# A four-layer S5/H3 stack on one core: pairwise scan, convolution first, layers chunk by chunk

## The chip, the cores and the metric

The kernel runs as one launch on one core of a Trainium2 chip. The metric is the device time of the launch in microseconds; several launches are timed and the median is given. TensorE (PE) multiplies matrices into PSUM, VectorE (DVE) and ScalarE (ACT) work on SBUF and PSUM, GpSimd (POOL) makes a few index tables, and SyncE (SP) issues every DMA, in order.

## The reference

Four layers act on x, 2048 tokens of 640 channels in bf16, with a residual each: A, B, A, B. Both A layers share their weights, and so do both B layers.

```python
def _A_ref(x, ...):                       # x is layer-normed: u
    Lam_bar = exp(dt * Lam);  B_bar = ((Lam_bar - 1) / Lam)[:, None] * Bmat
    Bu = einsum("bld,pd->blp", x, B_bar)  # complex, 640 states
    for t in range(L): h = Lam_bar * h + Bu[:, t]
    y = 2 * einsum("blp,dp->bld", hseq, Cmat).real + x * Dskip

def _B_ref(q, k, v, ...):                 # q is layer-normed x
    kv = (4-tap causal filter of k by shift_k) * v
    y = causal convolution of kv with ssm_k along 2048 tokens (by FFT of 4096)
    return q * (y + kv * ssm_D)

x = x + A(layernorm(x)); x = x + B(layernorm(x)); x = x + A(layernorm(x)); x = x + B(layernorm(x))
```

The convolution Y = y + kv * ssm_D does not depend on x: it is computed once and used by both B layers.

## The kernel before

A list scheduler (class `Sched`) is given tasks with engines, estimated durations, dependencies and a priority; it plays them through and emits their instructions in the order of their planned starts. So the order on each engine is fixed in the program and comes from the planner's numbers. Buffers come from `Ring`s whose slots are assigned in the order in which tasks are written down.

The program has two parts, each with its own schedule.

*Part 1* holds the setup of A's weights (`a_setup_tasks`), the DFT tables (`y_table_tasks`), the preparation of kv and of the filter (`kv_tasks`), the convolution, and layer A1, planned together. `kv_tasks` treats 128 channels at a time. k is transposed in by DMA, filtered by four diagonal matmuls (L884), multiplied by v on DVE (L893), and stored to `kvs`. The filter `ssm_k` is transposed in by DMA (L837), rearranged by ACT (L845) and stored to `ksx`. `y_pass_builders` then runs five passes of 128 channels: load K and V by DMA transpose (L993, L1008), stage A (L936), stage B (L964 to L971), the spectral product on DVE (L1030 to L1035), the inverse (L1062 to L1066), a DMA transpose of `q` (L1084), the last inverse step (L1101), and a store to `ysc` (L1116). Evictions go to ACT (L249) or DVE (L251). All passes wait for a task `gate`:

```python
gate = S.add("gate", "pool", 0.0, [AT["bt"], AT["tab"], AT["w"], TK["inv"], TK["fa"]]
             + x_ready + kv_stores + kk_stores, e_gate)
```

*Part 2* loads the whole of Y (L1315) and runs B1, A2 and B2 over x, which stays in SBUF in f32.

Layer A (`a_layer_tasks`) works in chunks, of 256 tokens in A1 and of 512 in A2. LayerNorm: squares on ACT (L489), root (L495 to L500), application on ACT (L509) into `u`. A DMA transpose makes `uT` (L542). PE forms Bu (L557), ACT evicts it to `ab` (L563). The complex recurrence is run as two real scans: Bu is rotated by the angle of Lam_bar (DVE, L579 to L584), scanned, and rotated back into `h` (L625 to L630), with a carry between chunks. The scans are one per 128 states and per real or imaginary part:

```python
for c2 in range(2):
    for j in range(NJ):                                   # NJ = 5
        nc.vector.tensor_tensor_scan(g[:, c2, j, :], r[:, j:j + 1].to_broadcast([P, CH]),
                                     g[:, c2, j, :], init, ALU.mult, ALU.add)   # L594
```

PE multiplies `h` by C (L648), adds the skip by a diagonal matmul (L654) and the residual x by an f32 identity matmul (L657); ACT evicts the sum into x with its row sums (L665). Layer B (`b_apply_tasks`) multiplies the normed x by Y on DVE (L1145) and adds the residual (L1147, or L1150 into the output).

Of the kernel before, what the change touches and what calls it, by code (L numbers as in the profile page):

```python
# [17 lines left out]
P = 128  # L18
# [5 lines left out]
CHMAX = 512  # L24
# [5 lines left out]
HALF_PI = 0.5 * math.pi  # L30

# [10 lines left out]
class Task:  # L42
    __slots__ = ("name", "eng", "engs", "ests", "est", "deps", "emit", "idx", "start", "finish", "rank", "succ", "bias", "lat")

    def __init__(self, name, eng, est, deps, emit, idx, bias, lat):
        if isinstance(eng, (tuple, list)):
            self.engs = tuple(eng)
            self.ests = tuple(float(e) for e in est)
        else:
            self.engs = (eng,)  # L50
            self.ests = (float(est),)
# [6 lines left out]
        self.bias = bias  # L58
        self.lat = lat


class Sched:
    LAT = {"pe": 0.15, "act": 0.25, "dve": 0.2, "pool": 0.3, "sp": 2.0, "sp": 2.0}
# [6 lines left out]
    def add(self, name, eng, est, deps, emit, bias=0.0, lat=None):  # L70
        t = Task(name, eng, est, deps, emit, len(self.tasks), bias, lat)
        self.tasks.append(t)
        return t

    def vis(self, d):
        return d.finish + (d.lat if d.lat is not None else self.LAT.get(d.eng, 0.2))

    def run(self):
        tasks = self.tasks
        for t in tasks:  # L80
            for d in t.deps:
                d.succ.append(t)
        for t in reversed(tasks):
            t.rank = t.est + max((s.rank for s in t.succ), default=0.0) + t.bias
        eng_free = {}
        ndep = {t.idx: len(t.deps) for t in tasks}
# [8 lines left out]
        remaining = len(tasks)  # L95
        all_engs = sorted({e for t in tasks for e in t.engs})
        DMAQ = ()
        while remaining:
            progressed = False
            for eng in all_engs:  # L100
                if eng_free.get(eng, 0.0) > now + 1e-9:
                    continue
                if eng in DMAQ and eng_free.get("bus", 0.0) > now + 1e-9:
                    continue
                cands = [t for t in ready if eng in t.engs and rtime[t.idx] <= now + 1e-9]
                if not cands:
                    continue
                def okay(t):
                    return t.engs[0] == eng or eng_free.get(t.engs[0], 0.0) > now + 0.3
                cands = [t for t in cands if okay(t)]  # L110
# [8 lines left out]
                if eng in DMAQ:  # L119
                    eng_free["bus"] = t.finish  # L120
                order.append(t)
                remaining -= 1
# [8 lines left out]
            nxt = []  # L131
            for t in ready:
                for eng in t.engs:
                    f = eng_free.get(eng, 0.0)
                    if eng in DMAQ:
                        f = max(f, eng_free.get("bus", 0.0))
                    nxt.append(max(f, rtime[t.idx]))
            nxt = [x for x in nxt if x > now + 1e-9]
# [3 lines left out]
        assert len(order) == len(tasks), "dependency cycle"  # L142
        order.sort(key=lambda t: (t.start, t.idx))
        for t in order:
            t.emit()
        self.makespan = max(t.finish for t in tasks) if tasks else 0.0
        if self.debug and tasks:
            busy = {}
            for t in tasks:
                busy[t.eng] = busy.get(t.eng, 0.0) + t.est  # L150
            print("[sched] makespan %.1f  busy: %s" % (self.makespan, {k: round(v, 1) for k, v in busy.items()}))
            byeng = {}
            for t in order:
                byeng.setdefault(t.eng, []).append(t)
            pos = {t.idx: i for e in byeng.values() for i, t in enumerate(e)}
            t = max(tasks, key=lambda t: t.finish)
            chain = []
            while t is not None and len(chain) < 400:
                chain.append(t)
                cands = [(self.vis(d), d) for d in t.deps]  # L160
                i = pos[t.idx]
                if i > 0:
                    pv = byeng[t.eng][i - 1]
                    cands.append((pv.finish, pv))
                cands = [c for c in cands if abs(c[0] - t.start) < 1e-6]
                t = cands[0][1] if cands else None
            chain.reverse()
            last = None
            out = []
            for t in chain:  # L170
                out.append("%s@%.1f" % (t.name, t.start))
            print("[sched] critical chain (%d): %s" % (len(chain), " > ".join(out[:: max(1, len(out) // 60)])))
            bk = 20.0
            nb = int(self.makespan / bk) + 1
            engs = ["pe", "act", "dve", "pool", "sp", "sp"]
            occ = {e: [0.0] * nb for e in engs}
            for t in tasks:
                s0, e0 = t.start, t.finish
                b0 = int(s0 // bk)
                while s0 < e0 - 1e-9:  # L180
                    be = (b0 + 1) * bk
                    seg = min(e0, be) - s0
                    occ[t.eng][b0] += seg
                    s0 += seg
                    b0 += 1
            print("[sched] occupancy per %.0fus (pe act dve pool sp sq):" % bk)
            for b_ in range(nb):
                print("   %5.0f  " % (b_ * bk) + " ".join("%3.0f" % (100 * occ[e][b_] / bk) for e in engs))
        self.tasks = []
        return self.makespan  # L190


class Slot:
    __slots__ = ("tile", "users", "alloc")

    def __init__(self, alloc):
        self.tile = None
        self.users = []
        self.alloc = alloc

    def get(self):
        if self.tile is None:
            self.tile = self.alloc()
        return self.tile


class Ring:

    def __init__(self, bufs, alloc):
        self.bufs, self.alloc, self.slots = bufs, alloc, []  # L210

    def new(self):
        war = list(self.slots[-self.bufs].users) if len(self.slots) >= self.bufs else []
        s = Slot(self.alloc)
        self.slots.append(s)
        return s, war


def t_mm(n, f32=False):
    return (0.45 if f32 else 0.216) * n / 512.0 + 0.012  # L220


def t_act(n, sb=False):
    return 0.30 + (0.00083 if sb else 0.00076) * n


def t_tt(n, slow=False):
    return 0.06 + (0.00108 if slow else 0.00055) * n
# [1168 lines left out]
```

## Time and profile before

| | |
|---|---|
| timed runs | 586.04 us median of 3 (585.99 to 587.17) |
| profiled execution | span 583.7 us; its own time is not listed, so the 2.3 us around the span are taken from the median |
| PE busy | 370.4 us (63%), weight loads beside it 256.7 |
| DVE busy | 394.4 us (68%) |
| ACT busy | 339.1 us (58%) |
| POOL busy | 13.7 us (2%) |
| DMA | 44.81 MB, mean 77 GB/s |
| chain that ended last | DVE 43%, PE 25%, ACT 21%, DMA 6% |
| granted TensorE clock, mean | 0.860 |

In a row of groups stand the source line, engine, operation, written and read tiles, form and count; then busy us and mean ns of one; then the idle time of the engine just before them and what ended it. A slice row has 40 digits, each the busy tenths of a fortieth of the span.

### The profile page before, as it was taken

How to read it: one execution, taken by the hardware profiler on the slowest of the kernel's cores; microseconds unless marked ns; L12 is line 12 of the kernel's file. 1: busy time of each engine (PE TensorE's matmuls, PEld its weight loads, DVE VectorE, ACT ScalarE, POOL GpSimd, SP SyncE). 2: the span in 40 equal slices, each digit the busy share in tenths (PEclk: the TensorE clock that was granted, in tenths of full speed). 3: DMA queues.
4: the chain of work that ended last, by engine and by line, in shares of the span. 5: the costliest groups of instructions: out<-in, count | busy, mean ns of one | idle time of the engine just before them, and what ended most of it. 6: DMA issues, size and time to landing. Idle time of an engine off the chain costs nothing.

```text
span 583.7 us, 8215 instructions
## 1 busy us (share of the span) xinstructions
PE 370.4 (63%) x3233; PEld 256.7 (44%) x3233; DVE 394.4 (68%) x799; ACT 339.1 (58%) x584; POOL 13.7 (2%) x38
## 2 busy tenths in 40 slices
PE   0326557659989898898979510075496793970291
PEld 0225547437767776686766410032153251530050
DVE  5974445992956977868961513559999299729903
ACT  8979964237778755674645419995241621960033
POOL 4211000000000000000000000000000000000000
PEclk9999869889999998998989755577887797995596
DMA  8931898681335451423103154040002002110101
GB/s 256 173 77 47 190 244 201 180 199 37 73 60 108 60 111 24 95 55 79 37 1 73 37 107 182 4 86 2 0 0 46 0 2 45 46 45 0 45 1 45
DMA packets 124370, 44.81 MB, mean 77 GB/s; under 512 B 117543, under 2 KB 122924, under 8 KB 124204
## 3 DMA queue, kind: packets, MB, share of 16 engines
q1 hardware_dynamic: 124332, 44.29, 33.4%
q8 instruction: 25, 0.41, 0.3%
q14 instruction: 13, 0.11, 0.1%
HBM read 9.51 MB, written 10.49 MB: 34 GB/s over the span
## 4 chain that ended last, share of the span: by engine, by line
DVE 43%; PE 25%; ACT 21%; DMA 6%; issue 2%; SPq 2%; POOL 0%; DVEq 0%; ACTq 0%; POOLq 0%
DVE g L594 13%; PE pb L557 7%; PE pc L648 6%; ACT junk L489 6%; ACT q L249 4%; ACT bu L509 3%; PE pc L657 3%; DMA uT<-u 2%; ACT ab L563 2%; DVE bo L1150 2%; DVE g L581 2%; DVE t L579 2%; DVE t L582 2%; DVE t L580 2%; DVE t L626 2%
## 5 line engine op out<-in xcount | busy, mean ns | idle before, releaser
L648 PE MATMUL pc<-W,h 128*128 128x128 bf16 (+1 forms) x640 | 110.2, 316 | 61.5 <-DVE h L627 53.5
L557 PE MATMUL pb<-uT,BT 128*128 128x256 bf16 (+1 forms) x600 | 105.3, 328 | 63.5 <-ACT std L496 37.0
L249 ACT ACTIVATE q<-yps 128x1024 bf16<-128x1024 f32 (+2 forms) x104 | 95.9, 964 | 32.7 <-PE yps L971 16.9
L648 PEld LDWEIGHTS <-h 128*128 128x128 bf16 x640 | 52.9, 101 | 122.8 <-DVE h L627 66.3
L557 PEld LDWEIGHTS <-BT 128*128 128x128 bf16 x600 | 60.2, 103 | 88.3 <-DVE std L495 37.1
L594 DVE TENSOR_TENSOR_SCAN g<-r,ncarry,g 128x256 bf16<-128x256 f32 (+1 forms) x100 | 82.3, 890 | 0.0
L665 ACT ACTIVATE x<-pc 128x640 f32<-128x640 f32 x32 | 22.4, 701 | 97.9 <-PE pc L657 97.8
L489 ACT ACTIVATE junk<-x,nmean 128x640 bf16<-128x640 f32 x64 | 52.2, 816 | 22.3 <-DVE nmean L483 22.3
L563 ACT ACTIVATE ab<-pb 128x512 bf16<-128x512 f32 (+1 forms) x60 | 43.7, 737 | 34.9 <-PE pb L557 15.4
L657 PE MATMUL pc<-x,ident_f 128*128 128x128 f32 (+1 forms) x128 | 48.5, 461 | 0.0
L251 DVE CAST q<-yps 128x256 bf16<-128x256 f32 (+1 forms) x11 | 7.9, 715 | 53.4 <-PE yps L1066 18.1
L509 ACT ACTIVATE u<-x,nmr,rstd 128x640 bf16<-128x640 f32 x32 | 27.9, 911 | 17.9 <-DVE nmr L500 6.7
L968 PE MATMUL yps<-q,Cf 128*128 128x128 bf16 x150 | 34.1, 228 | 2.6 <-ACT q L249 1.9
L971 PE MATMUL yps<-q,Cf 128*128 128x128 bf16 x150 | 34.3, 229 | 0.0
L970 PE MATMUL yps<-q,NSf 128*128 128x128 bf16 x150 | 34.2, 228 | 0.0
L969 PE MATMUL yps<-q,Sf 128*128 128x128 bf16 x150 | 34.2, 228 | 0.0
L884 PE MATMUL yps<-DS,kT 128*128 128x128 bf16 x320 | 25.4, 253 | 11.2 <-DVE kx L893 9.1
L884 PEld LDWEIGHTS <-kT 128*128 128x128 bf16 x320 | 24.4, 116 | 18.0 <-issue 16.2
L483 DVE TENSOR_SCALAR nmean<-sums 128x1 f32<-128x1 f32 x64 | 7.5, 148 | 34.0 <-ACT x L665 23.6
L509 ACT ACTIVATE bu<-x,nmr,rstd 128x640 bf16<-128x640 f32 x32 | 28.2, 909 | 1.9 <-DVE bo L1150 1.1
L579 DVE TENSOR_TENSOR t<-ab,cs 128x1280 bf16<-128x1280 bf16 (+1 forms) x12 | 12.5, 1043 | 21.4 <-ACT ab L563 21.4
L1145 DVE TENSOR_TENSOR bu<-bu,Y 128x640 bf16<-128x640 bf16 x32 | 15.5, 488 | 16.4 <-ACT bu L509 16.4
(202 smaller groups left out, 746.3 us busy)
## 6 DMA issues: line engine op xcount, KB each, us to landing
xb<-in_A_x_dram SPq DMA_DIRECT2D x8, 320.0 KB, 4.2
vb<-in_B_v_dram SPq DMA_DIRECT2D x5, 512.0 KB
kvs<-kx SPq DMA_DIRECT2D x5, 512.0 KB, 6.3
ksx<-kx SPq DMA_DIRECT2D x5, 512.0 KB
ysc<-yq SPq DMA_DIRECT2D x5, 512.0 KB, 4.0
Y<-ysc SPq DMA_DIRECT2D x1, 2560.0 KB
out_dram<-bo SPq DMA_DIRECT2D x4, 640.0 KB
Bin<-in_A_B_re_dram SPq DMA_DIRECT2D x1, 800.0 KB
```

The source lines that it names most:

```text
L249: nc.scalar.activation(out, in_, ACT.Copy)
L489: nc.scalar.activation(junk[:], x[:, a, :], ACT.Square, bias=st["nmean"][:, k:k + 1], scale=1.0, accum_out=st["ssq"][:, k:k + 1])
L509: nc.scalar.activation(dst, src, ACT.Identity, bias=st["nmr"][:, k:k + 1], scale=st["rstd"][:, k:k + 1])
L557: nc.tensor.matmul(pb[:, c2, :], lhsT=BT[:, (c2 * NJ + j) * NJ + k, :], rhs=uTv()[:, k, :], start=(k == 0), stop=(k == NJ - 1))
L563: nc.scalar.activation(s_ab.get()[:, :, j, :], s_pb.get()[:], ACT.Copy)
L594: nc.vector.tensor_tensor_scan(g[:, c2, j, :], r[:, j:j + 1].to_broadcast([P, CH]), g[:, c2, j, :], init, ALU.mult, ALU.add)
L648: nc.tensor.matmul(pc[:, d0:d1], lhsT=h[:, c2, j, tsl], rhs=W[:, c2, j, d0:d1], start=first, stop=False)
L657: nc.tensor.matmul(pc[:, d0:d1], lhsT=consts["ident_f"][:], rhs=x[:, a, d0:d1], start=False, stop=True)
L884: nc.tensor.matmul(pk[:, a4 * P:(a4 + 1) * P], lhsT=kT[:, t0:t0 + P], rhs=s_ds.get()[:, l, :], start=(l == 0), stop=(l == 3))
L969: nc.tensor.matmul(ps[:, g, 0, :], lhsT=T["Sf"][:, q, :], rhs=aim, start=False, stop=True)
L970: nc.tensor.matmul(ps[:, g, 1, :], lhsT=T["NSf"][:, q, :], rhs=are, start=True, stop=False)
L971: nc.tensor.matmul(ps[:, g, 1, :], lhsT=T["Cf"][:, q, :], rhs=aim, start=False, stop=True)
```

## The change

The kernel is largely rewritten. In part 1 stand now only setup and the convolution of all channels; in part 2 all four layers, chunk by chunk (four chunks of 512 tokens; `tok_view` puts token pairs into one partition row), planned together. Its planner assigns ring slots as it plays tasks through. There is no gate.

*Pairwise scan.* With Lam = lambda, the state after the odd token of pair b obeys H[b] = lambda^2 H[b-1] + (B u[odd] + lambda B u[even]). `BT0` (B transposed by DMA) and `BT1` (lambda-scaled) give the bracket; a scan runs over the 256 pairs of a chunk. The odd token's output is W0 H[b] + D u; the even one's is W1 H[b-1] + G0 u, with W1 = C lambda and G0 = C B + D; the factor of B_bar and the 2 lie in W0 and W1, made by matmuls in setup. The five state blocks of a part lie end to end, and one scan runs over all 5 x 258 elements: the table `rtab` holds 0 at a block's first place, 1 at its second, then |lambda|^2.

```diff
 e_ri
-    nc.vector.tensor_tensor(t1v, ab[:, 0], CS, ALU.mult)      # and five more, N5 = 5 * CH
+    nc.vector.tensor_tensor(t1[:, :, :, 0:NB], ab[:, 0, None].to_broadcast(sh), tab[:, 0:2, :, 2:NC2], ALU.mult)
+    nc.vector.tensor_tensor(t2[:, :, :, 0:NB], ab[:, 1, None].to_broadcast(sh), tab[:, 1:3, :, 2:NC2], ALU.mult)
+    nc.vector.tensor_tensor(g[:, :, :, 2:NC2], t1[:, :, :, 0:NB], t2[:, :, :, 0:NB], ALU.add)
 e_sc
-    for j in range(NJ):
-        nc.vector.tensor_tensor_scan(g[:, c2, j, :], r[:, j:j + 1].to_broadcast([P, CH]), ...)
+    rt = aw["rtab"][:].rearrange("p j b -> p (j b)")
+    for c2 in range(2):
+        gv = g[:, c2].rearrange("p j b -> p (j b)")
+        nc.vector.tensor_tensor_scan(gv, rt, gv, 0.0, ALU.mult, ALU.add)
 e_ro
-    (six tensor_tensor of N5)
+    nc.vector.tensor_tensor(t1[:], g[:, 0, None].to_broadcast(sh), tab[:, 0:2], ALU.mult)
+    nc.vector.tensor_tensor(t2[:], g[:, 1, None].to_broadcast(sh), tab[:, 1:3], ALU.mult)
+    nc.vector.tensor_tensor(h[:], t1[:], t2[:], ALU.add)
 e_bp
-    nc.tensor.matmul(pb[:, c2, :], lhsT=BT[...], rhs=uTv()[:, k, :], ...)         # 50 of CH columns
+    nc.tensor.matmul(pb[:, jj, c2, :], lhsT=aw["BT1"][:, c2, j, k, :], rhs=uT[:, k, 0:2, :]...)     # even tokens
+    nc.tensor.matmul(pb[:, jj, c2, :], lhsT=aw["BT0"][:, c2, k, j * P:(j + 1) * P], rhs=uT[:, k, 2:4, :]...)  # odd
 e_cp
-    nc.tensor.matmul(pc[:, d0:d1], lhsT=consts["ident_f"][:], rhs=x[:, a, d0:d1], start=False, stop=True)
+    if par: ops = ops + [(uT[:, k, slot, :], aw["DD"][:, k, :], ...) for k in ...]
+    else:   ops = [(uT[:, k, slot, :], aw["G0"][:, k, d0:d1], d0, d1) for k in range(NJ)] + ops
 e_xe
-    nc.scalar.activation(x[:, a, :], s_pc.get()[:], ACT.Identity, accum_out=sums[:, a:a + 1])
+    nc.vector.scalar_tensor_tensor(xs()[:, q, :], s_pc.get()[:, 0:D], 1.0, resid(q), ALU.mult, ALU.add,
+                                   accum_out=sums_out()[:, q:q + 1])
 kv_tasks, y_pass
-    nc.sync.dma_start_transpose(out=s_kn.get()[:], in_=B_ssm_k[kb * P:(kb + 1) * P, :])   # then ACT, then store to ksx
-    nc.sync.dma_start_transpose(out=s_xk.get()[:], in_=ksx[...])
-    nc.sync.dma_start_transpose(out=s_xv.get()[:], in_=kvs[...])
-    nc.tensor.matmul(pk[...], lhsT=kT[:, t0:t0 + P], rhs=DS[:, l, :], ...)                # 320 of 128 columns
+    nc.sync.dma_start_transpose(out=s_vT.get()[:], in_=B_v[0][:, kb * P:(kb + 1) * P])
+    nc.tensor.matmul(pk[...], lhsT=DS[:, l, :], rhs=kT[:, t0:t0 + 512], ...)              # 80 of 512 columns
+    nc.sync.dma_start(out=s_xk.get()[:], in_=rows(B_ssm_k[c0:c0 + DQ, :]))
+    nc.sync.dma_start(out=s_xv.get()[:], in_=rows(kvd[c0:c0 + DQ, :]))
 part 2
+    for c in range(NCH): A1.chunk(c, ...)
+    for c in range(NCH): b_chunk(..., "B1", ...); A2.chunk(c, ...)
+    for c in range(NCH): b_chunk(..., "B2", ...)
```

The LayerNorm application may now stand on ACT or DVE, as the planner chooses; x comes in bf16 chunks (`xb`, L1176) whose row sums are taken on ACT (L1182); Y comes in chunks (L1196). The convolution's PSUM ring has four slots of 1024 columns, shared with everything else in the part (two before).

How the order changes is shown at three places. The first is DVE in one chunk of layer A. Before, in A2 (512 tokens):

```order
L579 TENSOR_TENSOR t_4883<-ab,cs 128x2560
L580 TENSOR_TENSOR t_4884<-ab,sn 128x2560
L495 TENSOR_SCALAR std<-ssq 128x4
L581 TENSOR_TENSOR g<-t_4883,t_4884 128x2560
L483 TENSOR_SCALAR nmean<-sums 128x1
L498 RECIPROCAL rstd<-std 128x4
L582 TENSOR_TENSOR t_4883<-ab,cs 128x2560
L583 TENSOR_TENSOR t_4884<-ab,sn 128x2560
L594 SCALAR_TENSOR_TENSOR g<-r,ncarry,g 128x512
L584 TENSOR_TENSOR g<-t_4883,t_4884 128x2560
L594 SCALAR_TENSOR_TENSOR g<-r,ncarry,g 128x512 x9
```

Now, for the third chunk of A1 (the rows L665 and L667 between are B1 of the second chunk):

```order
L575 TENSOR_TENSOR t1_3395<-ab_3340,tab_100 128x10x256
L576 TENSOR_TENSOR t2_3396<-ab_3340,tab_100 128x10x256
L667 SCALAR_TENSOR_TENSOR x1_3095,sums_3524<-bu_3497,x1_3095 128x640
L577 TENSOR_TENSOR g_3394<-t1_3395,t2_3396 128x10x256
L665 TENSOR_TENSOR bu_3499<-bu_3499,Y_2577 128x640
L591 SCALAR_TENSOR_TENSOR g_3394<-rtab_101,g_3394 128x1290 x2
L603 TENSOR_TENSOR nca_3568<-g_3394,ctab_102 128x10
L614 TENSOR_TENSOR t1_3576<-g_3394,tab_100 128x2580
```

Six rotations of 2560 and ten scans of 512 have become three of 2560 and two scans of 1290 (the order names scans by their instruction class).

The second is DVE between the second and the third chunk of A1. Before (ncarry is the carry, q a tile of the convolution):

```order
L609 TENSOR_TENSOR ct<-g,snC_99 128x5
L610 TENSOR_TENSOR ct<-g,csC_98 128x5
L630 TENSOR_TENSOR h<-t_1858,t_1859 128x1280
L611 TENSOR_TENSOR ncarry<-ct 128x5
L251 CAST q_1364<-yps 128x4x32x8
L251 CAST q_1563<-yps 128x4x32x8
L579 TENSOR_TENSOR t_2022<-ab,cs 128x1280
L580 TENSOR_TENSOR t_2023<-ab,sn 128x1280
```

Now (x0 and x1 are the first two chunks, u_3210 is the normed input of the third):

```order
L667 SCALAR_TENSOR_TENSOR x0_2951,sums_3146<-bu_3197,x0_2951 128x640
L488 TENSOR_SCALAR nmean_3216<-sums_3146 128x4
L499 TENSOR_SCALAR std_3199<-ssq_3179 128x4
L502 RECIPROCAL rstd_3202<-std_3199 128x4
L641 SCALAR_TENSOR_TENSOR x1_3095,sums_3096<-ps_3152,xb_2573 128x640
L504 TENSOR_TENSOR nmr_3204<-nmean_3178,rstd_3202 128x4
L488 TENSOR_SCALAR nmean_3219<-sums_3096 128x4
L513 TENSOR_SCALAR u_3210<-xb_3055,rstd_3202,nmr_3204 128x5x128
```

Before, the third chunk's rotation follows the second's with only convolution work between, since its LayerNorm stands earlier. Now its LayerNorm stands behind B1 of the first chunk and among the residuals of the second.

The third is SP where part 1 ends. Before:

```order
L1084 DMA_TRANSPOSE q_4183<-q_4138 128x32x128
L1116 DMA ysc<-yq 2048x1x128
L1315 DMA Y<-ysc 128x10240
L542 DMA_TRANSPOSE uT<-u 128x20x128 x4
L1158 DMA out_dram<-bo 128x4x640 x4
L1392 UNCONDITIONAL_BRANCH
```

Now:

```order
L1046 DMA ysd_81<-yq_2459 128x16x128
L1196 DMA Y_2575<-ysd_81 128x2x1280
L1196 DMA Y_2577<-ysd_81 128x2x1280
L1196 DMA Y_2579<-ysd_81 128x2x1280
L1176 DMA xb_2571<-in_A_x_dram 128x2x1280
L1176 DMA xb_2573<-in_A_x_dram 128x2x1280
L538 DMA_TRANSPOSE uT_2622<-u_2615 128x20x128
```

The x loads, which stood at the start of the program, now stand behind the last store of the convolution and three loads of Y.

More of the change, by code (lines that the diff above doesn't have):

```diff
@@ L141, in run @@
             now = min(nxt)
-        assert len(order) == len(tasks), "dependency cycle"
+        assert len(order) == len(tasks), "no order: " + " ".join(t.name for t in ready[:20])
         order.sort(key=lambda t: (t.start, t.idx))
         for t in order:
[L145 to L188, printed above, removed]
@@ L910, in y_pass_builders, with y_pass @@
+    return stores, t_dsl, st
+def y_pass(S, nc, R, T, TK, R_ps, kdst, t_kd, B_ssm_k, kvd, ysd, kv_store, qd):
     c0 = qd * DQ
-    st = {}
-    tab_f = [TK["sin"], TK["fa"], gate]
-    q1, q2, q3, qx, R_y = rings
     H = {}
```

1622 lines of the change are left out of this document (754 added, 868 removed).

## Prediction

> **What bounds the kernel now.** I read the page's slices first, then the stage windows, then the groups by form for prices, and last the chain and the timeline for order. The slices:
>
> ```profile
> span 583.7 us, 8215 instructions
> ...
> DVE  5974445992956977868961513559999299729903
> ACT  8979964237778755674645419995241621960033
> PEclk9999869889999998998989755577887797995596
> DMA  8931898681335451423103154040002002110101
> ```
>
> No engine is full throughout; the bound changes by stage. The windows (columns: stretch, length, busy time of PE, PEld, DVE, ACT, POOL, granted clock, DMA share, GB/s) cut at the events I use:
>
> ```profile
> 0.00:62.00 62.00, 20.89 (x204) 19.18 (x205) 42.55 (x218) 53.88 (x130) 13.41 (x36) 1.00 0.59 138
> 62.00:126.00 64.00, 38.90 (x381) 30.89 (x378) 41.75 (x95) 34.09 (x57) 0.28 (x3) 0.87 0.88 206
> 126.00:347.00 221.00, 185.10 (x1986) 145.69 (x1986) 146.73 (x217) 138.35 (x190) 0.00 (x0) 0.93 0.34 66
> 347.00:397.00 50.00, 14.11 (x60) 6.19 (x61) 23.32 (x94) 45.55 (x87) 0.00 (x0) 0.61 0.32 89
> 397.00:584.00 187.00, 111.38 (x606) 54.73 (x604) 140.02 (x179) 67.24 (x122) 0.00 (x0) 0.80 0.08 22
> ```
>
> ```profile
> 124.93 2.07 SPq L993 DMA_TRANSPOSE qx<-ksx  x1
> ```
>
> The convolution's first load is issued at 124.93: the gate holds it until all setup, kv and filter work is stored, under 88% DMA load. Then convolution and A1 share the chip until 347 (PE 185.10 of 221, 84%). From 397 DVE leads (140.02 of 187, 75%) through the four 512-token chunks of A2.
>
> **Prices.** By form (busy us, mean ns of one, idle before):
>
> ```profile
> L594 DVE TENSOR_TENSOR_SCAN g<-r,ncarry,g 128x256 bf16<-128x256 f32 x70 | 46.4, 729 | 0.0
> L594 DVE TENSOR_TENSOR_SCAN g<-r,ncarry,g 128x512 bf16<-128x512 f32 x30 | 35.9, 1266 | 0.0
> L594 DVE TENSOR_TENSOR_SCAN g<-r,g 128x512 bf16<-128x512 f32 x10 | 11.4, 1202 | 0.0
> L594 DVE TENSOR_TENSOR_SCAN g<-r,g 128x256 bf16<-128x256 f32 x10 | 5.9, 655 | 0.0
> L627 DVE TENSOR_TENSOR h<-t,t 128x1280 bf16<-128x1280 bf16 x8 | 6.6, 822 | 0.1
> L627 DVE TENSOR_TENSOR h<-t,t 128x2560 bf16<-128x2560 bf16 x4 | 6.0, 1491 | 0.0
> L1030 DVE TENSOR_TENSOR q<-q,q 128x2176 bf16<-128x2176 bf16 x5 | 6.5, 1292 | 6.8 <-ACT q L249 6.6
> L893 DVE TENSOR_TENSOR kx<-yps,vb 128x512 bf16<-128x512 f32 x20 | 13.5, 685 | 10.5 <-PE yps L884 4.9 <-DMA vb<-in_B_v_dram 3.2 <-DMA kvs<-kx 2.5
> L1150 DVE TENSOR_TENSOR bo<-bu,x 128x640 bf16<-128x640 bf16 x16 | 13.2, 825 | 0.4
> L1145 DVE TENSOR_TENSOR bu<-bu,Y 128x640 bf16<-128x640 bf16 x32 | 15.5, 488 | 16.4 <-ACT bu L509 16.4
> L258 DVE TENSOR_SCALAR sct_rr_t<-sct_rr_t 128x256 f32<-128x256 f32 x10 | 3.1, 308 | 0.1
> L606 DVE TENSOR_TENSOR ct<-g,csC 128x5 f32<-128x5 bf16 x10 | 1.6, 159 | 0.0
> L251 DVE CAST q<-yps 128x1024 bf16<-128x1024 f32 x4 | 4.9, 1225 | 19.0 <-PE yps L936 15.1 <-issue 3.9
> L249 ACT ACTIVATE q<-yps 128x1024 bf16<-128x1024 f32 x91 | 89.2, 1023 | 21.7 <-PE yps L971 16.9 <-PE yps L1066 2.1 <-PE yps L936 2.1
> L437 ACT ACTIVATE BT<-yps 128x640 bf16<-128x640 f32 x10 | 6.7, 685 | 0.1
> L489 ACT ACTIVATE junk<-x,nmean 128x640 bf16<-128x640 f32 x64 | 52.2, 816 | 22.3 <-DVE nmean L483 22.3
> L665 ACT ACTIVATE x<-pc 128x640 f32<-128x640 f32 x32 | 22.4, 701 | 97.9 <-PE pc L657 97.8
> ```
>
> A PE mean holds the pipeline's tail, so PE is priced by spacing, from runs of ten (chain and timeline); the third row below came after 37 us of rest:
>
> ```profile
> 249.85 1.09 PE pb L557 x10
> 513.45 2.16 PE pc L648 x10
> 382.89 5.82 PE pb L557 x20
> ```
>
> ```profile
> 240.39 0.72 PE L648 MATMUL pc<-W,h 128*128 128x128 bf16 x10
> ```
>
> That is 0.109 us for 256 columns, 0.216 for 512, and for 128 at most 0.072; since 256 takes 0.109, I take 0.056. After the rest the 512-column matmuls took 0.291 each.
>
> **The second stage (four layers, chunk by chunk), DVE.** The scan costs (1266-729)/256 = 2.10 ns an element and 0.19 us an instruction. Before: 46.4+35.9+11.4+5.9 = 99.6 us. After: 16 scans of 1290, 2.90 each, 46.4: 53 less. Its multiplier is now a stored f32 table, not a broadcast column; no row has that, so I take the old rate and bound it by twice that (+46). Rotations: twelve kinds, x8 at 0.82 and x4 at 1.49, 150 us before; now 48 at 1.50, 72: 78 less. The residual moves to DVE: 32 scalar_tensor_tensor of 640 at about 0.82 (L893's 685 for 512, extended; L1150's 825 agrees), 26 more. Per A chunk: rotations 9.0, scans 5.8, residual 3.3, small ones 1.5 (0.16 each): 19.6, times 8 is 157. Per B chunk 4 x (0.49+0.82) and 0.7: 5.9, times 8 is 47. 23 of the LayerNorm applications now stand on DVE: 0.31 to 0.82 each (L258, L1150), I take 0.5: 11. Sum 215.
>
> PE: per A chunk 100 matmuls of 256 (10.9), two even tiles of 15 x (0.216+0.056) and two odd of 10 x 0.272 + 5 x 0.056, 14.1; 25 in all, 200 over 8 chunks. The added G0 products replace the f32 identity matmuls at about the same cost. ACT loses L665 (22.4) and gains 16 sums of about 0.8: with 64 squares (52), 24 evictions of up to 1.02 (22) and 41 applications of at most 1.0 it holds about 128 us and binds nowhere.
>
> Neither 215 nor 200 is the stage's length, since layers of one chunk follow each other. Transfers on its path, by the tile's answer, the issue list and the chain:
>
> ```profile
> DMA to landing us min/median/max: 4.8/4.8/4.8
> ```
>
> ```profile
> xb<-in_A_x_dram SPq DMA_DIRECT2D x8, 320.0 KB, 4.2
> ```
>
> ```profile
> 336.80 6.70 DMA q<-q
> 346.74 4.04 DMA ysc<-yq
> 62.38 6.28 DMA kvs<-kx
> ```
>
> I walked the written order by hand, from the first x chunk's landing at 0. Chunk 0: four sums 3.1, four squares 3.3 (0.82 each), root and one function table 3, application 2, transpose 4.8: first matmul at 17. Bu ends at 29 (rested PE), its last eviction at 30; rotation in 4.4, scans 5.6, rotation out with carry 5: state at 45. Chunk 1's state follows at 62, its output at 76, B1 of chunk 0 at 79. Only then does DVE's queue reach the row that finishes chunk 2's LayerNorm, although its x could be loaded by 69: PE rests from 76 to 88, DVE nearly too until 101. Then DVE is almost full: states of A1 at 119 and 137, of A2 at 164, 188, 206 and 235 (each 15.5 of rotation and scan plus the residuals and B1/B2 products between them). The last output takes 14 on PE (250), then residual, squares, root, application, product and store 14: 264. DVE's 215 thus leaves 49 open: 30 at the head, some 10 around 90, the rest mostly at the tail.
>
> **The first stage (setup and convolution).** DVE, by counts in the order: 43 casts 41, 30 spectral products 39, 10 kv products at 1.2, the rest setup, 139. ACT: 117 evictions of 0.69 to 1.02, 108, in all 124. PE: per pass 32 x 0.109 + 224 x 0.056 = 16, times 5 is 80; kv 80 x 0.216 = 17; lambda-scaled B 6; W0/W1 20 x 2 x 0.272 = 11; G0 14: 128. The DFT table FA stands behind some 45 small DVE operations (7 us), 12 of up to 0.9 on 768 (7), 10 on 256 (3) and 6 diagonals (1.5): about 24 with the parameter load. From there three engines hold about 115 to 128 us each. At the 84% that PE reached from 126 to 347 this is 152: the last G0 matmul at 176. The first V load waits for a kv store (6.3) behind it on SP, and K of pass 1 waits behind that load; until then K0 and four kv blocks cover it, and without that cover it would cost up to 10. The gate's 125 us go, since nothing now waits for all of setup.
>
> The loads of filter and kv: before, the filter was transposed in, rearranged on ACT, stored, and transposed back, kv the same but for the first step (15 transposes of 512 KB, 10 stores). Now the filter is read once as it lies, kv is stored and read once as it lies, v is transposed in (5), and B in natural form (10 short ones). That is less for SP and the DMA engines in a stage whose DMA share was 34% once the gate was open, so I cost it at nothing; the cover is the 128 us of PE work, and if a load is late it is the V load above. The PSUM ring of the convolution has four slots instead of two; its gain, if any, lies inside the 84%. A1 moves behind the convolution with all that it issues: its x loads (8 of 320 KB become 4 of 640) and transposes (8 become 4) now stand on SP behind the Y loads.
>
> At the boundary SP issues ysd's last store, three Y loads, then x; x also waits for G0, whose B tile lies where x goes. A store is 4.0 and x 4.2, and Y's 1.9 MB rides beside it; 6 after G0: x at 182.
>
> Sum: 182 + 264 + 2.3 around the span (median 586.04 less 583.7) = 448; 4 for hand-overs the walk took at zero: **452 us**.
>
> The step-0 reads of `ab` and `g` on DVE speak against the sum if they run at half rate; the rival below prices that. The Trainium skill (Vector Engine (DVE) Microarchitecture Reference, 5.1 Performance modes) says that a row read again and again with step 0 still ran two elements a cycle with two sources; no row of this trace shows such a read.
>
> **Rivals.** *Overlap stays as loose as before.* To 347 PE was busy 245 of 347, 71%: 24+128/0.71+6 = 210. From 347 DVE was busy 163 of 237, 69%: 215/0.69 = 312. Total 524. For it: the chunk-by-chunk carry chain; against: two chunks and two layers fill each other's gaps in the written order. Chance 0.12.
> *Broadcast rotations at one element a cycle.* L1150 gives (825-150)/640 = 1.05 ns, so 2.85 instead of 1.49 for 32 products: +44, 496. Chance 0.07; a slow scan table (+46) lands at the same place and shares it.
> *Slower than before: PE stays at a low clock through the second stage.* PE's 200 would double to 400 and bind: 182+17+400+15+2 = 616. It decides (586) once the mean clock there is under 0.54. Against it: 0.80 from 397 to 584 with PE 60% busy, and here it is 200 of 264; for it: 0.61 from 347 to 397. Chance 0.03. The Trainium skill (TensorE: Matmul & The Clock Gate, Part 1) has PE at half clock after a window of about 3.4 us without work, until as long a stretch of work; by that rule some eight pauses of the walk would each cost up to 1.7, an estimate of 14 in place of the 5 that the walk holds. The quoted run after a rest agrees in kind (0.291 against 0.216).
> *No gaps at all.* 24+128+6, then 264 less the pause near 90: about 414. Chance 0.06.
>
> **How the numbers follow.** Main case 0.72, spread 418 to 490 by the first stage's share (71 to 100%) and the walk. The range 418 to 508 takes in the second rival and leaves out the first, third and most of the fourth: about 0.8. Faster by over 0.2% (about 1.2 us, what a measurement can tell) 0.96, within it 0.01, slower 0.03.
>
> **What would show it.** Right: 16 scans near 2.9, rotations near 1.5, no gate pause, G0's last matmul near 176, x landing near 182, DVE about 215 in what follows, a PE pause of about 12 between chunk 1's output and chunk 2's Bu. Wrong: a scan over 4 us, a rotation over 2.5, or a second stage over 300 with DVE under 70%.

## The result, and the profile after

| kernel | median us | ratio to before, 95% interval |
|---|---|---|
| before | 586.61 | |
| changed | 461.95 (461.25 to 463.44) | 0.7876 [0.7858, 0.7894] |

The change takes 124.7 us off; forecast were 452 and a range of 418 to 508, so it lies within the range and 10 above the forecast. The profiled execution spans 460.6 at a mean clock of 0.914 (0.860 before). Its page, busy times and slices:

```profile
span 460.6 us, 7946 instructions
...
PE 349.6 (76%) x3303; PEld 256.2 (56%) x3330; DVE 323.9 (70%) x595; ACT 244.9 (53%) x380; POOL 6.9 (1%) x21
...
PE   0386777989888796049799529999997698999920
...
DVE  4995657688787630022997715999699899699674
```

In 349.6 us of work PE still does nearly what it did (370.4); DVE falls from 394.4 to 323.9. Two dips stand out on PE, the 17th digit (the boundary between the two parts: x's load and first LayerNorm) and the 24th (the pause before chunk 2). The windows, cut at 24 us, where the prediction put the DFT table FA (it was made at 21.2), and at the last G0 matmul (columns as in the prediction):

```profile
24.00:181.00 157.00, 132.12 (x1623) 104.83 (x1630) 104.66 (x174) 103.08 (x120) 0.34 (x3) 0.96 0.75 156
181.00:461.00 280.00, 211.76 (x1663) 148.85 (x1680) 201.45 (x326) 130.00 (x243) 0.00 (x0) 0.88 0.19 50
```

The first part ran PE at 132.12 of 157 us, 84%. In the second, PE (76%) is as busy as DVE (72%): neither alone fills it. The groups by form on DVE in that stretch, which answer the scans, rotations, residuals and LayerNorm applications of the prediction:

```profile
L591 DVE TENSOR_TENSOR_SCAN g<-rtab,g 128x1290 bf16<-128x1290 f32 x16 | 44.8, 2833 | 0.0
...
L641 DVE SCALAR_TENSOR_TENSOR x<-ps,x 128x640 f32<-128x640 f32 x16 | 13.0, 816 | 0.0
...
L575 DVE TENSOR_TENSOR t<-ab,tab 128x2560 bf16<-128x2560 bf16 x8 | 11.9, 1492 | 15.5 <-ACT ab L562 15.5
...
L513 DVE TENSOR_SCALAR u<-x,rstd,nmr 128x640 bf16<-128x640 f32 x8 | 7.1, 933 | 0.1
```

The chain through the boundary, in order of time (start, length, what):

```profile
177.04 3.29 PE ps L464 x30
...
180.38 3.97 DMA xb<-in_A_x_dram
...
197.35 4.87 DMA uT<-u
...
202.36 1.23 PE ps L553 x5
```

### The profile page after: what moved, and what is told of

Same layout as the page of the kernel before. It is cut to its first block, busy times and chain, and to the rows that moved or that the text cites. A ratio compares the mean times of both kernels' runs of the same rounds, so it can differ in the third digit from the quotient of the medians.

```text
span 460.6 us, 7946 instructions
## 1 busy us (share of the span) xinstructions
PE 349.6 (76%) x3303; PEld 256.2 (56%) x3330; DVE 323.9 (70%) x595; ACT 244.9 (53%) x380; POOL 6.9 (1%) x21
## 3 DMA queue, kind: packets, MB, share of 16 engines
q1 hardware_dynamic: 118138, 42.75, 41.8%
## 4 chain that ended last, share of the span: by engine, by line
DVE 38%; ACT 13%; PE 13%; DMA 5%; issue 2%; ACTq 0%; SPq 0%
DVE g L591 10%; ACT junk L494 8%; DVE x L641 4%; PE ps L464 3%; DMA xb<-in_A_x_dram 3%; DVE bu L665 2%; PE ps L553 2%; DVE t L575 2%; DVE o L670 2%; DVE g L577 2%; DVE t L615 2%; DVE t L614 2%; DVE t L576 2%; DMA uT<-u 2%; PE ps L556 2%; DVE x L667 2%
## 5 line engine op out<-in xcount | busy, mean ns | idle before, releaser
L636 PE MATMUL ps<-W,h 128*128 128x512 bf16 (+1 forms) x632 | 98.1, 304 | 6.4 <-DVE h L616 5.9
L223 ACT ACTIVATE q<-ps 128x1024 bf16<-128x1024 f32 (+2 forms) x81 | 75.4, 1003 | 42.8 <-PE ps L935 19.2
L553 PE MATMUL ps<-uT,BT 128*128 128x256 bf16 x400 | 61.1, 287 | 42.1 <-DMA uT<-u 41.8
L556 PE MATMUL ps<-uT,BT 128*128 128x256 bf16 x400 | 60.1, 284 | 0.0
L591 DVE TENSOR_TENSOR_SCAN g<-rtab,g 128x1290 bf16<-128x1290 f32 x16 | 44.8, 2833 | 0.0
L225 DVE CAST q<-ps 128x1024 bf16<-128x1024 f32 (+2 forms) x34 | 30.4, 929 | 17.2 <-PE ps L1009 10.4
L511 ACT ACTIVATE bu<-x,nmr,rstd 128x640 bf16<-128x640 f32 x26 | 23.5, 915 | 28.2 <-DVE x L667 18.4
L930 PE MATMUL ps<-q,Cf 128*128 128x128 bf16 x170 | 35.6, 222 | 3.5 <-DVE vT L872 2.8
L933 PE MATMUL ps<-q,NSf 128*128 128x128 bf16 x170 | 35.8, 222 | 0.0
L935 PE MATMUL ps<-q,Cf 128*128 128x128 bf16 x150 | 33.2, 221 | 0.0
L932 PE MATMUL ps<-q,Sf 128*128 128x128 bf16 x150 | 33.2, 221 | 0.0
L866 PE MATMUL ps<-kT,DS 128*128 128x512 bf16 x78 | 21.4, 431 | 14.4 <-DVE DS L845 11.3
L908 PE MATMUL ps<-FA,qx 128*128 128x256 bf16 x160 | 21.5, 276 | 9.1 <-DMA qx<-kvd 2.4
L636 PE MATMUL ps<-G,uT 128*128 128x128 bf16 (+1 forms) x151 | 26.8, 297 | 0.5
L908 PEld LDWEIGHTS <-qx 128*128 128x128 bf16 x160 | 15.6, 99 | 13.9 <-issue 9.0
```

What stands on the lines that cost most here:

```text
L223: nc.scalar.activation(out, in_, ACT.Copy)
L225: nc.vector.tensor_copy(out, in_)
L553: nc.tensor.matmul(pb[:, jj, c2, :], lhsT=aw["BT1"][:, c2, j, k, :], rhs=uT[:, k, 0:2, :].rearrange("p t i -> p (t i)"), start=(k == 0), s ...
L556: nc.tensor.matmul(pb[:, jj, c2, :], lhsT=aw["BT0"][:, c2, k, j * P:(j + 1) * P], rhs=uT[:, k, 2:4, :].rearrange("p t i -> p (t i)"), star ...
L591: nc.vector.tensor_tensor_scan(gv, rt, gv, 0.0, ALU.mult, ALU.add)
L636: nc.tensor.matmul(pc[:, o0:o1], lhsT=lh, rhs=rh, start=(n == 0), stop=(n == len(ops) - 1))
```

## The experiments

Differences are to the changed kernel's 461.95 unless said otherwise. Line numbers of the variants are shifted by a few lines.

| kernel | median us | ratio to before, 95% interval |
|---|---|---|
| before, half the recurrence | 528.14 | 0.8986 [0.8960, 0.9012] |
| scans twice | 500.94 | 0.8527 [0.8509, 0.8545] |
| gate put back | 494.73 | 0.8418 [0.8396, 0.8441] |
| transposed loads | 473.66 | 0.8086 [0.8062, 0.8111] |
| residual on PE and ACT | 471.81 | 0.8058 [0.8033, 0.8083] |
| D's addition on GpSimd | 469.06 | 0.8007 [0.7994, 0.8019] |
| scans per block | 462.19 | 0.7891 [0.7867, 0.7914] |
| x early, first try | 459.85 | 0.7828 [0.7803, 0.7853] |
| x early | 447.68 | 0.7646 [0.7623, 0.7670] |
| no scans | 443.31 | 0.7575 [0.7544, 0.7605] |
| three x buffers | 439.80 | 0.7510 [0.7472, 0.7549] |
| and statistics by tile at the end | 436.42 | 0.7454 [0.7441, 0.7467] |

### What the smaller recurrence alone is worth

The theory: the change gains by less DVE work and, as much, by its new order. The rival: the smaller recurrence is nearly all of it. In the kernel before, only the columns of all rotations and scans are halved (two lines shown of those changed):

```diff
-            nc.vector.tensor_tensor(t1v, ab[:, 0], CS, ALU.mult)              # all 12 rotations alike
+            nc.vector.tensor_tensor(t1v, ab[:, 0, :, 0:CH // 2], CS, ALU.mult)
-  tensor_tensor_scan(g[:, c2, j, :], r[:, j:j + 1].to_broadcast([P, CH]), ...)
+  tensor_tensor_scan(g[:, c2, j, 0:CH // 2], r[:, j:j + 1].to_broadcast([P, CH // 2]), ...)
```

> The kernel before, in its own order, with rotations and scans over half of each chunk's columns only; PE reads the states of the first half twice, the second half of the recurrence is left out. DVE loses 38 us of scans and about 64 of rotations, 102 in all, half of it in A1, which runs beside the convolution. Theory (the smaller recurrence pays only where DVE leads, from 397 on; before that PE and the gate set the pace): about 45 us less, 535 to 550. Rival (the smaller recurrence alone makes nearly the whole gain): 480 to 500.

Measured: 528.14, 59.4 us less than the kernel before (587.50 beside it): outside the theory's 535 to 550, and far from the rival's 480 to 500. DVE lost 103.1 us (394.4 to 291.3), so 58% of it showed. The tile of Y's store dates the end of the first part, before and then with half the recurrence:

```profile
L1116 SPq DMA_DIRECT2D ysc<-yq x5: 512/513/619, 184.5 to 346.7; - x5
```

```profile
L1116 SPq DMA_DIRECT2D ysc<-yq x5: 512/513/619, 179.7 to 329.6; - x5
```

Of the gain 17.1 lie before the last store, where the theory had nothing: A1's recurrence also held up the part that PE fills to 84%. The other 40.6 of the span lie behind it. So in the old order the smaller recurrence gives about half of the 124.7.

### The gate

```diff
-        t_kl = S.add(f"yq{qd}_kl", "sp", 0.1, [], e_kl, ...)
+        t_kl = S.add(f"yq{qd}_kl", "sp", 0.1, gate, e_kl, ...)   # gate: all of setup, tables, five kv stores; V alike
```

> The changed kernel with the gate put back: the loads of filter and kv for the convolution wait for all of the setup, the tables and the five kv stores, as before; the written order is planned anew with that. Theory (overlap of setup and convolution is a large part of the gain of the first stage): the first load goes at 85 to 125 us, then 80 us of convolution matmuls at 84% and some 12 of load and last inverse: the first stage ends at 190 to 232 in place of 180, the whole takes 475 to 515. Rival (the gate cost little, since the first stage is bound by the same sum of work on three engines): 462 to 467.

Measured: 32.8 us more, as the theory has it. The convolution's matmuls with FA (L908) and the first sum over x, in the changed kernel and then behind a gate (count, ns min/median/max, first and last start):

```profile
L908 PE MATMUL ps<-FA,qx x160: 269/272/417, 28.0 to 137.3; 128*128 128x256 bf16 x160
```

```profile
L1182 ACT ACTIVATE junk<-xb x16: 719/736/737, 184.7 to 273.2; 128x640 bf16<-128x640 bf16 x16
```

```profile
L908 PE MATMUL ps<-FA,qx x160: 269/272/421, 95.0 to 180.0; 128*128 128x256 bf16 x160
```

```profile
L1183 ACT ACTIVATE junk<-xb x16: 721/737/738, 217.8 to 306.3; 128x640 bf16<-128x640 bf16 x16
```

The convolution starts 67.0 us later and ends the part 33.1 later: half of the delay is made good (G0's matmuls, which end the part in the changed kernel, are done from 81 to 95 here), and all of what is left goes into the time.

### The layout of the loads

```diff
-            nc.sync.dma_start(out=s_xk.get()[:], in_=rows(B_ssm_k[c0:c0 + DQ, :]))
+            nc.sync.dma_start_transpose(out=s_xk.get()[:], in_=B_ssm_k[c0:c0 + DQ, :])     # kvd alike
```

> The changed kernel with the ten loads of filter and kv as DMA transposes of the same 512 KB again, in the same written order; the filter's rearrangement on ACT and its extra store and load are not put back, and the data lie in another order than the convolution wants. Each issue holds the queue about 2.3 us in place of 0.5. Theory (the loads are hidden, as the prediction had it): 460 to 465. Rival (the layout of the loads is a large part of the first stage's gain; the first stage waits for each load): 470 to 485.

Measured: 11.7 us more; the prediction's "cost at nothing" falls. The first and the last load of kv on the DMA queue (start, time that the issue holds the queue), in the changed kernel and with transposes:

```profile
38.63 0.38 SPq L967 DMA_DIRECT2D qx<-kvd  x1
...
117.20 0.36 SPq L967 DMA_DIRECT2D qx<-kvd  x1
```

```profile
42.94 2.82 SPq L967 DMA_TRANSPOSE qx<-kvd  x1
...
128.11 1.99 SPq L967 DMA_TRANSPOSE qx<-kvd  x1
```

The first is 4.3 late, the last 10.9, and the first sum over x 12.7 (197.4): each pass loses a little. DVE's wait for the filter at L956 doubles (waits of the two; total, times, longest):

```profile
DVE qx L956 <- DMA qx<-in_B_ssm_k_dram: 5.7, 4, 3.0
```

```profile
DVE qx L956 <- DMA qx<-in_B_ssm_k_dram: 11.9, 3, 5.6
```

To see whether this wait in DVE's queue is the way to the path, L956 went to GpSimd:

```diff
-            nc.vector.tensor_tensor(xk[:, :, 0], xk[:, :, 0], kdst["kd"][...], ALU.add)
+            nc.gpsimd.tensor_tensor(xk[:, :, 0], xk[:, :, 0], kdst["kd"][...], ALU.add)
```

> The changed kernel with the addition of D to the filter's first tap (L956, five of 128x16) on GpSimd instead of DVE, planned anew. In the changed kernel DVE stands 5.7 us at it waiting for the filter's loads, with kv products and evictions behind it; with transposed loads it stood 11.9 us and the whole took 11.7 more. Theory (the waits in DVE's queue are how the loads reach the path): 2 to 6 us less, 456 to 460. Rival (the matmuls wait for the same loads anyway): 461 to 464.

Measured: 7.1 us more, outside both. The order was planned anew and is another one: PE now comes to the first filter matmul before the table FA is made and rests there, and the first part ends 7.5 later (first sum over x at 192.2).

```profile
PE ps L908 <- DVE FA L770: 13.5, 1, 13.5
```

That rest explains little of it: the changed kernel's PE rests 11.3 us at the same place for another table (`DS`), and its first matmul there starts only 2.1 us earlier (19.07 against 21.18). So this run doesn't tell the two apart. Whether the held queue or the wait on DVE carries the 11.7 stays open.

### How much of DVE's work lies on the path

```diff
+                nc.vector.tensor_tensor_scan(gv, rt, gv, 0.0, ALU.mult, ALU.add)     # a second time
```

> The changed kernel with each of the 16 scans issued twice in a row on the same tile, everything else in the same written order; the recurrence is thus applied twice. 16 x 2.83 us = 45.3 us more on DVE. Theory (in the second stage DVE's work lies on the path nearly throughout, also at the head, where each state waits for its scan): 462 + 40 to 46 = 502 to 508. Rival (DVE is idle some 60 us of the second stage, and PE and the transposes set the length): the idle time takes up half or more, 470 to 485.

Measured: 39.0 us more, 86% of 45.3 and one us short of the theory's band; the rival is out. In this order DVE, idle for 79 of the 280 us, still takes hardly any added scan work for free. That does not mean that less work would be worth as much:

```diff
-                nc.vector.tensor_tensor_scan(gv, rt, gv, 0.0, ALU.mult, ALU.add)
```

> The changed kernel with its 16 scans left out, so that the recurrence is missing, in the same written order: 44.8 us less on DVE. Theory A (DVE alone sets the pace; doubling the scans cost 39.0): about 39 less, 423 to 428. Theory B (PE, with 212 us in the second stage and its rests at the head, before chunk 2 and in the tail, lies close behind DVE, which is why taking 16 us from DVE and giving 20 to PE in resid_pe made the time 9.9 longer): PE takes over, 181 + 20 + 212 + some 22 of the rest before chunk 2 + 15 of tail = 450; 440 to 452.

Measured: 18.6 us less, theory B. The windows of the second part without scans:

```profile
181.00:441.00 260.00, 205.43 (x1663) 146.63 (x1680) 158.72 (x310) 130.18 (x243) 0.00 (x0) 0.90 0.21 55
```

DVE is down to 61%, PE up to 79%. The chain that ended last, in the changed kernel and without scans:

```profile
DVE 38%; ACT 13%; PE 13%; DMA 5%; issue 2%; ACTq 0%; SPq 0%
```

```profile
PE 35%; ACT 13%; DVE 12%; DMA 6%; issue 2%; ACTq 0%; SPq 0%
```

So PE takes over, as theory B says. The sum in that expectation is looser than it looks. It took the longest wait of a row, 22.0, for the rest before chunk 2; the timeline below shows that this one is the head's, and that the rest is 13.75 (10.1 without scans). With PE's 205.4, a rest of 10.1 and the 2 around the span the sum gives 434, some 10 under the 443.3 measured, and these 10 were not followed up.

The residual, back on PE and ACT, points the same way:

```diff
+                    ops = ops + [(ident(), resid(q)[:, d0:d1], d0, d1)]      # bf16 in A1, f32 in A2
-                nc.vector.scalar_tensor_tensor(xs()[:, q, :], s_pc.get()[:, 0:D], 1.0, resid(q), ALU.mult, ALU.add, accum_out=...)
+                nc.scalar.activation(xs()[:, q, :], s_pc.get()[:, 0:D], ACT.Identity, accum_out=...)
```

> The changed kernel with the residual back where it was: PE adds x by an identity matmul (in bf16 for the first layer, whose x is bf16, in f32 for the third) and ACT evicts with the row sums; planned anew. DVE loses 32 x 0.82 = 26 us, ACT gains 32 x 0.7 = 22, PE about 22. Theory (DVE sets the pace of the second stage, PE has room): 15 to 22 us less, 440 to 447. Rival (PE, 76% busy there, takes DVE's place, and the extra hop PE to ACT to DVE is longer): 460 to 470.

Measured: 9.9 us more, the rival (its 460 to 470 passed by 2). The second part's window, the identity matmuls in f32, and the new wait:

```profile
181.00:470.00 289.00, 232.24 (x1776) 159.83 (x1776) 185.23 (x270) 145.97 (x299) 0.00 (x0) 0.91 0.19 49
```

```profile
L638 PE MATMUL ps<-x,ident_f 128*128 128x512 f32 x32 | 16.8, 606 | 0.0
```

```profile
ACT x L644 <- PE ps L638: 42.2, 12, 8.6
```

PE took 20.5 us more, DVE gave 16.2, and ACT, now a step between PE and DVE, waited 42.2 for PE. The order was planned anew, so that the added work, the extra step and the order are not told apart.

### One scan or five

```diff
-                nc.vector.tensor_tensor_scan(gv, rt, gv, 0.0, ALU.mult, ALU.add)
+                for j in range(NJ):
+                    nc.vector.tensor_tensor_scan(g[:, c2, j, :], aw["rtab"][:, j, :], g[:, c2, j, :], 0.0, ALU.mult, ALU.add)
```

> The changed kernel with five scans of 258 elements for each part in place of one of 1290, in the same written order: 64 more scans at about 0.19 us of fixed cost, 12.2 us more on DVE. Theory (86% of work added to DVE's scans shows in the time, as the doubled scans gave 39.0 of 45.3): 471 to 474. Rival (the fixed cost of a scan overlaps with the scan before it): 462 to 466.

Measured: 462.19, the rival: no difference. The ten scans of a chunk in a row against the two, from the timelines (start, length, instruction, count), and the group of the ten:

```profile
221.66 5.98 DVE L590 TENSOR_TENSOR_SCAN g<-rtab,g 128x258 bf16<-128x258 f32 x10
```

```profile
L590 DVE TENSOR_TENSOR_SCAN g<-rtab,g 128x258 bf16<-128x258 f32 x80 | 48.2, 672 | 0.0
```

```profile
220.86 5.58 DVE L591 TENSOR_TENSOR_SCAN g<-rtab,g 128x1290 bf16<-128x1290 f32 x2
```

Ten of 672 ns take 5.98 us, not 6.72: 74 ns of each lie under the next. Eight scans more cost 0.40 us, 50 ns each, not the 190 that the prediction read from the difference of two durations. By that the merging is worth 3.2 us of DVE (64 times 50 ns); of what the scans save, the halved columns are nearly all.

### The head and the pause

```diff
-            "xb": ring(2, p1, ...), "u": ring(2, p1, ...)
+            "xb": ring(2, px, ...), "u": ring(2, px, ...)     # px: a pool over the space of the kv preparation
```

> The changed kernel with xb and u in a pool of their own, over the space of the kv preparation, which is free long before the convolution ends; the x loads then no longer wait for the last G0 matmul and stand ahead of the last stores on the DMA queue. Theory (the head of the second stage, 22 us from the last G0 matmul at 180.3 to the first Bu matmul at 202.4, is a plain chain of load, sums, squares, application and transpose): the chain up to the transpose runs beside the G0 matmuls, the transpose starts at about 181, the first Bu matmul at about 186; 445 to 449 us. Rival (something behind the head, DVE or the load of chunk 2, sets the end, and the head is slack): 456 to 462.

Measured: 2.1 less, a small gain (interval of the ratio 0.7803 to 0.7853, against 0.7858 to 0.7894): the rival's numbers, but not for its reason. x's load was issued at 139.7 in place of 180.4, and the first sum still waited (ACT's timeline; idle before it in brackets):

```profile
182.64 0.74 ACT L1185 ACTIVATE junk<-xb 128x640 bf16<-128x640 bf16 x1 [2.14 <-PE ps L468]
```

L468 closes the last G0 product. The sum writes a scratch tile, `junk`, and its result into a small tile, and both still lay on space of the setup. So the second try moved `junk`, the small tiles and g too; which of them held the sum is not told apart:

> As x_early, and now the sums' scratch tile junk, the LayerNorm's small tiles and g also lie on space that is free before the last G0 matmul, since in x_early the first sum still started only at 182.6, behind that matmul. Theory (the head is on the path): sums and squares of chunk 0 run between 172 and 181, beside the G0 matmuls; the transpose starts at 181 to 183 and the first Bu matmul at 186 to 188 in place of 202; all that follows moves with it: 445 to 450 us. Rival (what follows is paced by something the head doesn't move): 455 to 462.

Measured: 14.3 less, the theory. First Bu matmul at 188.1 in place of 202.4:

```profile
L553 PE MATMUL ps<-uT,BT x400: 269/273/421, 188.1 to 386.6; 128*128 128x256 bf16 x134
```

All 14.3 us saved at the head arrive at the end. Then the rest before chunk 2 (12.50 us in this kernel), whose x waits for chunk 0's residual to free its buffer:

```diff
-            "xb": ring(2, px, ...), "Y": ring(3, p0, ...)
+            "xb": ring(3, px, ...), "Y": ring(2, p0, ...)
```

> As x_early2, with three x buffers and two of Y instead of two and three, so that chunk 2's x no longer waits for chunk 0's residual; the order is planned anew. Theory (PE's 22 us wait for chunk 2's transposed u, and DVE's idle time there, lie on the path): the wait goes, 10 to 16 us less than x_early2: 430 to 438. Rival (DVE's work is only moved, and the idle time comes back later, in the tail): within 4 of x_early2, 443 to 450.

Measured: 439.80, 7.9 less than the kernel with x early (447.68), between theory and rival. PE no longer rests before chunk 2; of the 12.50 us under two thirds arrive at the end. PE's waits for transposed u, 41.8 us in the changed kernel and 25.8 with x early, are down to 18.2, of which 8.6 are the head's:

```profile
PE ps L553 <- DMA uT<-u: 18.2, 4, 8.6
```

Last, the LayerNorm statistics of the last chunk tile by tile:

```diff
+    if out is not None and c == NCH - 1: st, posts = ln_each(...)     # mean, square, root for each q by itself
```

> As x_three2, and in the last chunk of B2 the LayerNorm statistics are taken for each of the four token tiles by itself, so that squares need not wait for the fourth residual; planned anew. In x_three2 DVE rests 3.9 us and the four squares stand in a row at 423.2 behind the last residual. Theory (the tail is a chain): 4 to 7 us less than x_three2's 439.8: 433 to 436. Rival (DVE is busy with chunk 2's products in the same stretch, and 12 more small operations eat the gain): 438 to 441.

Measured: 436.42, 3.4 less by the medians, just under the theory's band. In the profiled runs the stretch from the last matmul to the end fell by 4.2 us (18.4 to 14.2), while the newly planned first part had lost 1.6 (first Bu matmul at 191.05 against 189.41). The time lies 25.5 us (5.5%) under the changed kernel's.

## Why the prediction was right

*The first part, 176 forecast, 180.3 measured.* The share of 84% held to the digit (132.12 of 157). PE's sum was 132 from 24 us on, and 5.7 more before it, against 128 forecast: that is the 4.3. DVE and ACT, put at 115 to 128 from there on, had only 104.7 and 103.1. The 84% had been measured with A1 beside the convolution, other loads and two PSUM slots; that the same share came out without them was not derived, and is in part luck. x landed 4.0 after G0 ended (6 forecast), at 184.4 against 182. That it counts to have no gate is shown (32.8). That the loads in natural layout are worth nothing is refuted (11.7): the prediction compared DMA shares, and the added time showed on the queue and in each pass. The sum did not suffer from it, because the 84% was taken over as it stood; how much of that share the new loads held up was not tried.

*DVE's work, 215 forecast, 201.45 in the window.* Scans 44.8 (46.4), rotations 71.6 (72), residuals 25.9 (26) came as priced; both rivals on rates are out (2833 ns with a stored table; 1492 with a broadcast row, where the products before took 1489 without one). The Trainium skill (Vector Engine (DVE) Microarchitecture Reference, 5.1 Performance modes) has a row read with step 0 by a two-source operation at two elements a cycle; the 1492 ns agree. The 23 LayerNorm applications took 15.7, not 11, eight of them 933 ns. The rows of this stretch add up to 219, which is what the 215 should be held against. The window counts 201: the durations overlap, as the ten scans show, and a sum of them is some 8% too long.

*The walk, in us from x's landing.*

| event | forecast | measured |
|---|---|---|
| first Bu matmul | 17 | 18.0 |
| first rotation | 30 | 32.0 |
| states of chunks 0 and 1 | 45, 62 | 46.5, 62.2 |
| PE's rest before chunk 2 | 76 to 88 | 75.6 to 89.4 |
| rotation of chunk 2 | 101 | 105.2 |
| A1 states of chunks 2, 3 | 119, 137 | 121, 139 |
| A2 states | 164, 188, 206, 235 | 169, 195, 212, 241 |
| last residual (forecast: 250 and one residual) | 251 | 262 |
| end | 264 | 276.2 |

The rests and the first rotations after them, in the timelines of PE and DVE:

```profile
202.36 1.23 PE L553 MATMUL ps<-uT,BT 128*128 128x256 bf16 x5 [22.00 <-DMA uT<-u]
...
273.80 1.25 PE L553 MATMUL ps<-uT,BT 128*128 128x256 bf16 x5 [13.75 <-DMA uT<-u]
```

```profile
216.40 1.50 DVE L575 TENSOR_TENSOR t<-ab,tab 128x2560 bf16<-128x2560 bf16 x1 [13.00 <-ACT ab L562]
...
289.64 1.50 DVE L575 TENSOR_TENSOR t<-ab,tab 128x2560 bf16<-128x2560 bf16 x1
```

The rest before chunk 2 came where it was forecast, but another wait sets it. The prediction had chunk 2's x loaded by 69 and its LayerNorm held up by DVE's queue. The rows of SP, ACT and DVE:

```profile
249.22 0.37 SPq L1176 DMA_DIRECT2D xb<-in_A_x_dram  x1
...
254.56 0.74 ACT L1182 ACTIVATE junk<-xb 128x640 bf16<-128x640 bf16 x1 [1.29 <-DMA xb<-in_A_x_dram]
...
264.21 0.17 DVE L499 TENSOR_SCALAR std<-ssq 128x4 f32<-128x4 f32 x1 [0.41 <-ACT junk L494]
```

The load goes out at 249.22, as chunk 0's last residual ends and frees its buffer, and has landed by 254.5, 70 on the walk's clock. From there to the first matmul at 273.80 pass 19.3 us; at the head, where DVE had no other chunk's products to do, it was 18.0. When DVE comes to the row for chunk 2's root (264.21), it has to wait for ACT's squares. So DVE's queue and B1 cost little over 1 us, and the late load sets the rest; with a third x buffer (and a new order) the rest was gone. So the walk had the right time by the wrong wait, which is luck.

The end came 12.2 later than in the walk. By chunk 2's rotation 4.2 had gathered: from its first matmul 13 were forecast and 15.8 taken (14.0 at the head), with four applications of 933 ns on DVE and one on ACT ahead of the last eviction of `ab`. A1's states made half of it good, A2's were 5 to 7 late again, which was not followed up, and the last matmul ended at 441.1, 6.7 late. The tail added 4.4: the walk put the last outputs and the last residual one behind the other, but DVE multiplies chunk 2's outputs between chunk 3's residuals, so that the last residual ends 5.2 us after the last matmul, at 446.3. From there to the end 14.3 passed, where the walk's 14 had held the residual too:

```profile
446.29 0.08 DVE L641 DVE_READ_ACCUMULATOR x<-ps,x 128x1 f32 x1
446.41 0.17 DVE L488 TENSOR_SCALAR nmean<-sums 128x4 f32<-128x4 f32 x1
450.49 0.17 DVE L499 TENSOR_SCALAR std<-ssq 128x4 f32<-128x4 f32 x1 [3.91 <-ACT junk L494]
```

The 12 us of the walk, with 2.4 at the boundary, less the 4 set aside for hand-overs, are about the 10 by which 452 was low.

*The rivals.* Loose overlap (524) put x at 210 and DVE at 69% after it. The first part held 84%. In the second its share was close (72%); it came out long (312 against 276) mostly because the 215 are a sum of durations, where the window counts 201. PE at a low clock: 0.88 in the second part, far from 0.54. PE's 200 became 211.76; five rests of 2.6 us and more were followed by stretches at a lower clock (below), which by the granted clock cost some 9 us, where the walk held 5. No gaps (414): the gaps were there; taking away most of the head's wait, the rest before chunk 2 and part of the tail gave 436.

*Where the 124.7 went, part by part.* Half the recurrence in the old order 59; the gate 33; the loads 12 (as transposes; the extra stores and loads of the kernel before were not put back); the residual on DVE 10; the merged scans nothing. They were measured from different kernels and need not add up; the 11 left over were not tried apart.

## What to carry to other kernels

Where two engines stood at 72 and 76% of a stage, adding work to the one cost nearly all of it (39.0 of 45.3), and taking as much away gained less than half (18.6 of 44.8): ask for both directions before moving work from one to the other. A price per instruction taken from the difference of two durations (190 ns here) can hold time that lies under the next instruction; take it from the spacing in a row (50 ns). A pause that comes at the forecast time can still have another cause: look at what its first instruction waited for, and follow that back. Before an early load is counted as a gain, look at every tile that the first instructions behind it write, the scratch tiles too: here the first try gained 2.1 us and the second 14.3.

## What the runs showed of the hardware

Of ten scans in a row, 672 ns each, 74 ns of each lie under the next, and a scan more costs 50 ns. The Trainium skill (Perfetto Trace Analysis, Optimizing Scalar/DVE Operations) puts the fixed overhead of a DVE instruction on SBUF at some 60 ns of the engine's time, and the profiled latency at about twice that, since the half in which the write is acknowledged overlaps with the next instruction. The 50 and the 74 ns come near that; the prediction's 190 did not use it.

A DMA transpose of 512 KB held the issuing queue 2.5 us (medians 2.50 for the filter, 2.44 for kv) where a plain load of the same size held it 0.53 and 0.37, at nearly the same time to landing (medians for kv 5.2 and 4.7).

After the rests of 22.00 and 13.75 us PE ran slow for about 4.2 us (202.36 to 206.58 at the head; 0.21 us for 256 columns against 0.109), and each time some 2 us were lost. The two stretches in the windows (granted clock 0.50), then the two after shorter rests, of 3.27 and 2.64 us:

```profile
202.40:206.60 4.20, 4.20 (x21) 2.97 (x22) 1.00 (x2) 1.61 (x2) 0.00 (x0) 0.50 0.36 70
273.80:278.00 4.20, 4.20 (x20) 2.99 (x21) 0.17 (x1) 4.04 (x11) 0.00 (x0) 0.50 0.00 0
231.00:234.80 3.80, 3.80 (x10) 1.37 (x11) 3.73 (x5) 0.00 (x0) 0.00 (x0) 0.55 0.02 4
353.07:356.60 3.53, 3.52 (x11) 1.34 (x12) 2.47 (x8) 3.53 (x9) 0.00 (x0) 0.61 0.00 0
```

The Trainium skill (TensorE: Matmul & The Clock Gate, Part 1) has half the clock until about 3.4 us of work. The runs agree in kind, with a stretch somewhat longer.
